# A fused decode block: five attention steps as a loop on TensorE, loads of half the size, and a sigmoid made of exponentials

## The chip, the cores and the metric

The kernel runs on one core of a Trainium2 chip. The metric is the device time of one execution in microseconds; three runs are made and the median is taken.

## The reference

One token for each of two batch rows goes through a layer norm and then through two branches, which are multiplied:

```python
B, D = 2, 448;  Hq, Hkv, Sk, Dh = 16, 8, 4096, 256;  F = 1792

xn = layernorm(x)
q  = (xn @ wq) as 16 heads of 256
p  = softmax(q @ k_cache^T / 16)            # 2 query heads share one of 8 K/V heads
s  = (p @ v_cache) as one row of 4096 @ wo
g  = silu(((xn @ w_gate) * (xn @ w_up)) @ w_down)
out = x + s * g
```

Everything is float32. The K and V caches are 67 MB each, and the five weight matrices some 24 MB together.

## The kernel before

There are 16 attention steps, one for each pair of a K/V head `g` and a batch row `b` (step `i` has `g, b = divmod(i, 2)`). A step reads 4.19 MB of K and 4.19 MB of V. The host lays these out so that a step is 128 rows (partitions) of 8192 numbers of each, 32 KB a row.

**The work of a step.** `scores(i)` makes 16 products on TensorE (32 matmul instructions in the profile) and leaves 128 x 1024 scores in a pair of PSUM banks `s`. `softmax(i)` takes the maximum on VectorE (`m`), turns it by two small products through the PSUM bank `sm` into a maximum for each head (`mx`), subtracts it in an exponential on ScalarE (`p`, with the sum in `su`), and transposes the result on VectorE (`pT`). `values(i)` makes 16 products of `pT` with V into the PSUM bank `o`, and VectorE copies them to `ob`. The order of the steps on TensorE is values(i), scores(i+1), the small products of softmax(i+1), then values(i+1). `combine`, `divide`, `turn` and `project` bring `ob` through the output weights; `total` adds the sums of the softmax.

**The loads.** All are issued on SyncE's queue (SP) in the order of `plan`. `ring` has two buffers of 64 KB a partition, `slot` holds one set of weights. V of step i and K of step i+1 are one load, `vk[i]`, of 128 rows of 64 KB (8.39 MB), and go to the two buffers in turn. A load into a buffer waits until TensorE has read what was there: the load of step i+2 waits for scores(i+1). Between them come the weights: `wgu` behind step 0, `wdq` behind step 2, `wo` behind step 8. At the end come `last0` (K of step 15 and V of step 14, two loads of 32 KB rows) and `last1` (V of step 15 and the rest of `wo`, seven pieces).

**The other branch.** `ffn_in` and `ffn_out` follow steps 0 and 2. The gate is `y * sigmoid(y)`, with ScalarE's sigmoid.

**The order of the instructions.** `Flow` records every operation with what it reads and writes. `settle` works out which earlier operations each has to wait for, and `issue` writes all of them out, unrolled, each engine in the order of the record, with one semaphore per engine and one per load. All instructions thus have one line, 164, in the profile, and groups are told apart by their tiles.

Of the kernel before, what the change touches and what calls it, by code (L numbers as in the profile page):

```python
# [4 lines left out]
AF = mybir.ActivationFunctionType  # L5
OP = mybir.AluOpType
AX = mybir.AxisListType

B, D = 2, 448
# [17 lines left out]
EXTRA = 2 * NS + 1  # L27
LEFT = 64 - NS * SIDE
EPS = 1e-5


class Flow:
# [6 lines left out]
    def __init__(self, nc):  # L39
        self.nc = nc  # L40
        self.ops = []
        self.touched = {}
        self.engines = dict(PE=nc.tensor, DVE=nc.vector, ACT=nc.scalar, POOL=nc.gpsimd, SP=nc.sync)

    def __getattr__(self, engine):
        return Recorder(self, engine)
# [13 lines left out]
        return box[0] // 32 * 32, -(-box[1] // 32) * 32, box[2] // 512 * 512, -(-box[3] // 512) * 512  # L60

    def record(self, engine, call, writes, reads, dma=False):
        op = dict(engine=engine, call=call, needs=set(), wanted=False, dma=dma)
        at = len(self.ops)
        for ap, write in [(a, False) for a in reads] + [(a, True) for a in writes]:
            if ap.tensor.name not in self.touched:
                continue
            psum = ap.space == bass.MemoryType.PSUM
            for other, its, wrote in self.touched[ap.tensor.name]:
                o = self.ops[other]  # L70
                box = self.region(ap)
                alone = psum and o["engine"] != engine
                if alone:
                    box, its = self.shared(box), self.shared(its)
                if not (write or wrote or alone) or box[0] >= its[1] or its[0] >= box[1] or box[2] >= its[3]                         or its[2] >= box[3]:
                    continue
                if o["engine"] == engine and not o["dma"] and (engine == "PE" or not wrote):
                    continue
                op["needs"].add(other)
        for ap, write in [(a, False) for a in reads] + [(a, True) for a in writes]:  # L80
            log = self.touched.setdefault(ap.tensor.name, [])
            box = self.region(ap)
            if write:
                log[:] = [(o, b, w) for o, b, w in log
                          if not (box[0] <= b[0] and b[1] <= box[1] and box[2] <= b[2] and b[3] <= box[3])]
            log.append((at, box, write))
        self.ops.append(op)
        return at

    def settle(self):  # L90

        known = {e: {} for e in self.engines}
        count = {e: 0 for e in self.engines}
        for at, op in enumerate(self.ops):
            e = op["engine"]
            count[e] += 1
            op["lane"], op["n"] = (("dma", at), 1) if op["dma"] else (e, count[e])
            need = [self.ops[o] for o in sorted(op["needs"], reverse=True)]
            waits = {}
            for o in need:  # L100
                if known[e].get(o["lane"], 0) < o["n"]:
                    if any(w["knew"].get(o["lane"], 0) >= o["n"] for w in waits.values()):
                        continue
                    if o["lane"] not in waits or waits[o["lane"]]["n"] < o["n"]:
                        waits[o["lane"]] = o
            waits = {k: o for k, o in waits.items()
                     if not any(w is not o and w["knew"].get(k, 0) >= o["n"] for w in waits.values())}
            for o in waits.values():
                for k, n in o["knew"].items():
                    known[e][k] = max(known[e].get(k, 0), n)  # L110
                o["wanted"] = True
            op["waits"] = sorted(waits.values(), key=lambda o: o["lane"] == e)
            op["knew"] = {**known[e], op["lane"]: op["n"]}

    def issue(self, final):
        nc = self.nc
        self.settle()
        sems = {}
        for op in self.ops:
            if op["wanted"] and op["lane"] not in sems:  # L120
                sems[op["lane"]] = nc.alloc_semaphore(f"s{len(sems)}")
        done = nc.alloc_semaphore("done")
        marks = {}
        for op in self.ops:
            e = op["engine"]
            waits = [(sems[o["lane"]], o["mark"]) for o in op["waits"]]
            while len(waits) > 1:
                gate = self.engines[e].wait_ge(*waits.pop(0))
                if len(waits) > 1:
                    gate.wait_op(*waits.pop(0), "sem-ge")  # L130
            if op is self.ops[-1]:
                for w in waits:
                    self.engines[e].wait_ge(*w)
                op["call"]().then_inc(done, 16)
                nums = sorted(s.num for s in sems.values())
                assert nums == list(range(nums[0], nums[-1] + 1))
                self.engines[e].sem_clear(range(nums[0], nums[-1] + 1))
                self.engines[e].wait_ge(done, 16)
                self.engines[e].sem_clear(done)
                break  # L140
            made = op["call"]()
            for w in waits:
                made.wait_op(*w, "sem-ge")
            if op["wanted"]:
                step = 16 if op["dma"] else 1
                marks[op["lane"]] = op["mark"] = marks.get(op["lane"], 0) + step
                made.then_inc(sems[op["lane"]], step)


class Recorder:  # L150
# [14 lines left out]
        return add  # L165


def gated_decode_block(nc, x, first, vk, last0, last1, wq0, wqx, wdq, wo, wgu, out):
    flow = Flow(nc)
    PE, DVE, ACT, POOL, SP = [getattr(flow, e) for e in ("PE", "DVE", "ACT", "POOL", "SP")]  # L170
    names = iter(range(1000))
# [58 lines left out]
    plan("wq0", wq0)  # L230
    plan("k0", first)
    weights = {0: ("wg wu", wgu), 2: ("wd wq1", wdq), 8: ("wo", wo)}
    for i in range(LAST):
        plan(f"v{i} k{i + 1}", vk[i])
        if i in weights:
            plan(*weights[i])
# [157 lines left out]
    def ffn_out():  # L394
        ps = bank()
        for i in range(14):
            t = i % NT
            PE.matmul(ps[W * t:W * (t + 1), :D], hT[:, i], loaded["wd"][:, i * D:(i + 1) * D],
                             start=i < NT, stop=i >= 14 - NT)
        y = bank()  # L400
        spread(lift(ps), y, True, True)
        e = work["h"]()[:, :SL]
        ACT.activation(e, y[:, :SL], AF.Sigmoid)
        DVE.tensor_mul(gate, y[:, :SL], e)


    def scores(i):
        g, b = divmod(i, B)
        k = loaded[f"k{i}"].rearrange("p (h d c n) -> p h d c n", h=2, d=2, c=NT)
        q = qT[g // 4][:, b, g % 4].rearrange("p d r j -> p d (r j)")  # L410
        m = work["m"]()
        s = two()
        for h in range(2):
            for d in range(2):
                for c in range(NT):
                    PE.matmul(s[W * c:W * (c + 1), h, :], q[:, d], k[:, h, d, c, :], start=d == 0, stop=d == 1)
        DVE.tensor_reduce(m[:, 0:1], s, axis=AX.XY, op=OP.max)
        return s, m


    su = sbuf([128, N], "su")
# [2 lines left out]
        g, b = divmod(i, B)  # L424
        return b * 4 + g if g < 4 else 8 + (b * 3 + g - 4 if i < LAST else 6 + b)

    def softmax(i, s, m, pT=None):
        sm = bank("sm")
        PE.transpose(sm[:1, :128], m[:, 0:1], ident)
        mx = work["mx"]()  # L430
# [10 lines left out]
        return pT  # L441

    over = sbuf([128, N], "over")

    def total(lo, hi, add):

# [54 lines left out]
    ob = work["ob"]()  # L501
    oT0 = sbuf([128, 4, 2, REP, W], "oT0")
    oT2 = sbuf([128, 1, 2, REP, W], "oT2")
    ss = scores(0)
    issue(2)
    p = softmax(0, *ss)
    for i in range(LAST):
        g, b = divmod(i, B)
        o = bank("o")
        values(i, p, o)  # L510
        ss = scores(i + 1)

        issue(1 + (i + 1 in weights))
        DVE.tensor_copy(ob[:, place(i) % 8], o)
        if i == LAST - 1:
            total(8, 14, add_head)
            cb = combine(ob, 6)
        p = softmax(i + 1, *ss)
        if i == 7:
            total(0, 8, add_head)  # L520
            cb = combine(ob, 8)
            for n in range(B):
                turn(oT0, divide(cb[:, n * 256:(n + 1) * 256], 4 * n, 4 * n + 4), 0, n, 4)
            ob = work["ob"]()
        if i in (0, 2, 4, 8):
            if i == 0:
                ffn_in()
            if i == 2:
                ffn_out()
            if i == 4:  # L530
                query(1)
            if i == 8:
                project(oT0, 0, 0, EARLY)

    for n in range(B):
        turn(oT1, divide(cb[:, n * 192:(n + 1) * 192], 8 + 3 * n, 11 + 3 * n), 0, n, 3)
    ss = scores(LAST + 1)
    ps = [p]
    project(oT1, 4, EARLY, LATE)

    last = slot()
    p = softmax(LAST + 1, *ss, last[:, :1024].rearrange("p (h n) -> p h n", h=2))
    o = bank("o")
    values(LAST, ps[0], o)
    ps.append(p)
# [17 lines left out]
    DVE.tensor_mul(gate, acc[:, :SL], gate)  # L563
    DVE.tensor_add(gate, gate, xg)
    SP.dma_start(out, gate)
    flow.issue(out)


# [52 lines left out]
```

## Time and profile before

| | |
|---|---|
| median of 3 runs | 375.16 us (374.98 to 375.22) |
| the profiled execution, its time | 374.99 us |
| the profiled execution, its span | 373.7 us |
| TensorE busy with matmuls | 192.1 us (51%), 1388 matmuls and as many weight loads |
| VectorE, ScalarE, GpSimd busy | 72.9 us (19%), 25.9 us (7%), 1.7 us |
| HBM read | 158.56 MB, 424 GB/s over the span |
| granted TensorE clock, mean | 0.776 |

Times in a row of the timeline or of the chain are the start from the beginning of the span and the duration, both in us; behind `x` stands the number of instructions that are put together in the row, and in brackets the idle time of the engine before it and what ended it. In the rows of waits stand the total, the number and the longest. In the rows of loads stand the number, the size of one, and the median time from issue to landing.

### The profile page before, as it was taken

How to read it: one execution, taken by the hardware profiler on the slowest of the kernel's cores; microseconds unless marked ns; L12 is line 12 of the kernel's file. 1: busy time of each engine (PE TensorE's matmuls, PEld its weight loads, DVE VectorE, ACT ScalarE, POOL GpSimd, SP SyncE). 2: the span in 40 equal slices, each digit the busy share in tenths (PEclk: the TensorE clock that was granted, in tenths of full speed). 3: DMA queues.
4: the chain of work that ended last, by engine and by line, in shares of the span. 5: the costliest groups of instructions: out<-in, count | busy, mean ns of one | idle time of the engine just before them, and what ended most of it. 6: DMA issues, size and time to landing. Idle time of an engine off the chain costs nothing.

```text
span 373.7 us, 3019 instructions
## 1 busy us (share of the span) xinstructions
PE 192.1 (51%) x1388; PEld 50.8 (14%) x1388; DVE 72.9 (19%) x125; ACT 25.9 (7%) x40; POOL 1.7 (0%) x9
## 2 busy tenths in 40 slices
PE   0781468082645091848173656601718090808685
PEld 0220112020111020212010111100202020202122
DVE  2303021104040004050404050400211203030530
ACT  1001010001021001010101010100010101010121
POOL 0100000000000000000000000000000000000000
PEclk9988587667588576798867696985958676877999
DMA  8999899999999999999999999999999999999995
GB/s 322 449 480 435 375 441 449 449 437 433 392 475 435 442 407 428 437 435 442 442 437 428 428 430 422 455 437 435 428 428 428 430 442 449 437 389 431 428 413 221
DMA packets 4217, 158.81 MB, mean 425 GB/s; under 512 B 599, under 2 KB 857, under 8 KB 1241
## 3 DMA queue, kind: packets, MB, share of 16 engines
q1 hardware_dynamic: 4201, 158.62, 98.4%
q8 instruction: 11, 0.18, 0.2%
q14 instruction: 1, 0.01, 0.0%
q10 hardware_dynamic: 4, 0.00, 0.0%
HBM read 158.56 MB, written 0.06 MB: 424 GB/s over the span
## 4 chain that ended last, share of the span: by engine, by line
DMA 75%; PE 22%; DVE 1%; issue 0%; ACT 0%; POOL 0%; ACTq 0%; DVEq 0%
DMA ring<-vk 68%; PE s L164 11%; PE o L164 10%; DMA ring<-last 6%; DMA p<-x 2%; DVE pT L164 0%; DVE qT L164 0%; DVE st L164 0%; DVE oT L164 0%; PE wide L164 0%; ACT ob L164 0%; PE cb L164 0%; DVE gate L164 0%; POOL rstd L164 0%; ACTq L164 0%
## 5 line engine op out<-in xcount | busy, mean ns | idle before, releaser
L164 PE MATMUL o<-ring,pT 128*32 128x512 f32 x480 | 82.5, 850 | 121.4 <-DMA ring<-vk 121.4
L164 DVE TENSOR_REDUCE m<-s 128x1 f32<-128x1024 f32 x16 | 19.6, 1222 | 226.9 <-PE s L164 226.9
L164 PE MATMUL s<-ring,qT 128*32 128x512 f32 x512 | 59.5, 607 | 1.1 <-DVE qT L164 1.1
L164 PEld LDWEIGHTS o<-ring,pT 128*32 128x32 f32 x480 | 18.5, 149 | 175.8 <-DMA ring<-vk 125.8
L164 ACT ACTIVATE p<-s,m 128x1024 f32<-128x1024 f32 x16 | 17.8, 1116 | 321.0 <-DVE m L164 321.0
L164 DVE STREAM_TRANSPOSE pT<-p 128x1024 f32<-128x1024 f32 x15 | 18.7, 1245 | 19.1 <-ACT p L164 19.1
L164 PEld LDWEIGHTS s<-ring,qT 128*32 128x32 f32 x512 | 16.1, 112 | 41.5 <-issue 39.5
L164 PE MATMUL s<-slot,xnT 128*32 128x512 f32 (+1 forms) x96 | 14.4, 751 | 2.3 <-DMA slot<-wgu 2.3
L164 PE MATMUL sm<-ident,m 128*1 128x128 f32 x16 | 4.3, 270 | 19.0 <-DVE m L164 19.0
L164 DVE TENSOR_REDUCE mx<-sm 1x128 f32<-1x512 f32 x16 | 10.7, 670 | 2.9 <-PE sm L164 2.9
L164 PE MATMUL sm<-one,mx 1*128 1x1 f32 x16 | 3.7, 231 | 14.2 <-DVE mx L164 14.2
L164 DVE COPY ob<-o 128x512 f32<-128x512 f32 x14 | 9.5, 681 | 0.0
L164 PE MATMUL s<-slot,oT 20*32 20x512 f32 (+3 forms) x28 | 7.9, 593 | 0.0
L164 PE MATMUL s<-slot,hT 128*32 128x448 f32 x28 | 5.0, 827 | 3.1 <-DMA slot<-wdq 3.1
L164 PE MATMUL s<-ident,pT 2*128 2x2 f32 (+2 forms) x8 | 0.7, 203 | 10.4 <-DVE pT L164 10.4
L164 PEld LDWEIGHTS sm<-ident,m 128*1 128x1 f32 x16 | 1.3, 79 | 33.0 <-DVE m L164 32.4
L164 PE MATMUL wide<-slot,oT 128*32 128x448 f32 x48 | 4.9, 543 | 1.4 <-DMA slot<-wo 0.9
L164 PE MATMUL cb<-ob,add_blocks 128*32 128x512 f32 (+2 forms) x48 | 4.1, 456 | 2.4 <-DVE ob L164 1.6
L164 PE MATMUL s<-ring,slot 128*32 128x512 f32 x32 | 4.2, 600 | 1.7 <-DMA ring<-last 1.7
L164 PEld LDWEIGHTS s<-slot,xnT 128*32 128x32 f32 x96 | 3.3, 137 | 10.4 <-issue 8.0
L164 PEld LDWEIGHTS sm<-one,mx 1*128 1x128 f32 x16 | 2.4, 147 | 17.2 <-DVE mx L164 17.2
L164 ACT ACT_TABLE_LOAD x3 | 3.8, 1283 | 1.6 <-PEq L613 1.6
(63 smaller groups left out, 39.7 us busy)
## 6 DMA issues: line engine op xcount, KB each, us to landing
ring<-last SPq DMA_DIRECT2D x2, 4096.0 KB, 27.5
slot<-wdq SPq DMA_DIRECT2D x1, 6720.0 KB, 46.3
slot<-wgu SPq DMA_DIRECT2D x1, 6272.0 KB, 34.5
slot<-wo SPq DMA_DIRECT2D x1, 5376.0 KB, 41.3
ring<-first SPq DMA_DIRECT2D x1, 4096.0 KB, 20.7
slot<-wq SPq DMA_DIRECT2D x1, 3328.0 KB, 10.8
ring<-last SPq DMA_DIRECT2D x1, 2048.0 KB, 20.4
ring<-last SPq DMA_DIRECT2D x1, 1536.0 KB, 22.4
```

Source lines behind the costliest of these rows:

```text
L164: self.flow.record(self.engine, lambda: method(out, *args, **kw), writes, reads, name == "dma_start")
```

## The change

Steps 9 to 13 (`TURNS`) become five turns of a loop on TensorE. The other engines keep their unrolled code. Four things follow from it:

- An instruction in a loop has fixed addresses, so V and K of these steps always go to the same two halves of one `ring` buffer, in two loads of 32 KB rows each (`late`); V may be loaded once values of the step before are done, K once the scores before are done. The scores always go to one pair of PSUM banks, the maximum to `steady`, and ScalarE copies the query to `qc`.
- Waits within a turn become semaphores of their own (gates): TensorE waits for them in instructions of their own and counts them down again. What the first turn needs from ahead of the loop is awaited before it.
- `softmax(i)` is moved from the end of the step before to the head of the turn. For step 9 this puts it behind `project(oT0, ...)`, and `total` and `combine` after step 13 come ahead of softmax(14). After the loop, `two()` gives scores(15) the pair of banks that held the scores of the loop.
- `SLOT = 0` sets the loop's first instruction at the beginning of a block of 256 instructions.

Apart from the loop, the sigmoid is computed as `y * exp(min(y, 0)) / (1 + exp(-|y|))`, so that ScalarE uses no function but the exponential.

The core of the diff:

```diff
+TURNS = range(9, 14)
+SLOT = 0
...
+        def put(op):
+            engine = self.engines[op["engine"]]
+            await_all(engine, op["waits"][:-1])
+            for gate, n in op["gates"]:
+                engine.wait_ge(gate, n).then_inc(gate, -n)
             made = op["call"]()
...
+            elif name == "PE":
+                for op in todo:
+                    if op["turn"] is None:
+                        put(op)
+                    elif op is mine[0][0]:
+                        await_all(engine, self.ahead)
+                        with nc.Fori(0, len(mine), engines=[mybir.EngineType.PE], head_slot={mybir.EngineType.PE: SLOT}):
+                            for o in mine[0]:
+                                put(o)
...
-        e = work["h"]()[:, :SL]
-        ACT.activation(e, y[:, :SL], AF.Sigmoid)
-        DVE.tensor_mul(gate, y[:, :SL], e)
+        e = work["h"]()
+        up, low = e[:, :SL], e[:, SL:2 * SL]
+        DVE.tensor_scalar(up, y[:, :SL], 0.0, None, op0=OP.min)
+        DVE.scalar_tensor_tensor(low, up, 2.0, y[:, :SL], op0=OP.mult, op1=OP.subtract)
+        ACT.activation(e[:, :2 * SL], e[:, :2 * SL], AF.Exp)
+        DVE.tensor_scalar(low, low, 1.0, None, op0=OP.add)
+        DVE.reciprocal(low, low)
+        DVE.tensor_mul(gate, y[:, :SL], up)
+        DVE.tensor_mul(gate, gate, low)
...
-    for i in range(LAST):
-        g, b = divmod(i, B)
+    for i in range(TURNS[0]):
         o = bank("o")
         values(i, p, o)
-        ss = scores(i + 1)
-
-        issue(1 + (i + 1 in weights))
+        s = scores(i + 1, query_of(i + 1), two() if i + 1 < TURNS[0] else pairs[0])
+        issue(min(1 + (i + 1 in weights), len(todo) - 2))
         DVE.tensor_copy(ob[:, place(i) % 8], o)
...
+    tile = ring()
+    for i in TURNS:
+        flow.turn = i
+        at = 2 * (i - TURNS[0])
+        loaded[f"v{i}"], loaded[f"k{i + 1}"] = tile[:, :ROW], tile[:, ROW:]
+        p = softmax(i, s)
+        SP.dma_start(loaded[f"v{i}"], late[at])
+        o = bank("o")
+        values(i, p, o)
+        DVE.tensor_copy(ob[:, place(i) % 8], o)
+        SP.dma_start(loaded[f"k{i + 1}"], late[at + 1])
+        ACT.copy(qc, query_of(i + 1))
+        scores(i + 1, qc, s)
+    flow.turn = None
+    issue(2)
+    total(8, 14, add_head)
+    cb = combine(ob, 6)
+    p = softmax(LAST, s)
     for n in range(B):
         turn(oT1, divide(cb[:, n * 192:(n + 1) * 192], 8 + 3 * n, 11 + 3 * n), 0, n, 3)
-    ss = scores(LAST + 1)
+    s = scores(LAST + 1, query_of(LAST + 1), two())
```

More of the change, by code (lines that the diff above doesn't have):

```diff
@@ L42, in __init__ @@
         self.touched = {}
-        self.engines = dict(PE=nc.tensor, DVE=nc.vector, ACT=nc.scalar, POOL=nc.gpsimd, SP=nc.sync)
+        self.turn = None
+        self.engines = dict(POOL=nc.gpsimd, DVE=nc.vector, ACT=nc.scalar, SP=nc.sync, PE=nc.tensor)
     def __getattr__(self, engine):
@@ L62, in record @@
     def record(self, engine, call, writes, reads, dma=False):
-        op = dict(engine=engine, call=call, needs=set(), wanted=False, dma=dma)
         at = len(self.ops)
+        op = dict(engine=engine, call=call, needs=set(), wanted=False, dma=dma, turn=self.turn, gates=[])
+        op["place"] = engine, sum(o["turn"] == self.turn and o["engine"] == engine for o in self.ops) if self.turn is not None else at
         for ap, write in [(a, False) for a in reads] + [(a, True) for a in writes]:
@@ L110, in settle, with loop @@
                     known[e][k] = max(known[e].get(k, 0), n)
-                o["wanted"] = True
             op["waits"] = sorted(waits.values(), key=lambda o: o["lane"] == e)
             op["knew"] = {**known[e], op["lane"]: op["n"]}
-    def issue(self, final):
+    def loop(self):
+        turns = sorted({o["turn"] for o in self.ops if o["turn"] is not None})
+        mine = [[o for o in self.ops if o["engine"] == "PE" and o["turn"] == t] for t in turns]
+        by = {(o["turn"], *o["place"]): o for o in self.ops if o["turn"] is not None}
+        self.ahead = []
+        for n, same in enumerate(zip(*mine)):
+            gates = {o["place"] for op in same[1:] for o in op["waits"]}
+            assert all(o["turn"] == op["turn"] for op in same[1:] for o in op["waits"])
+            self.ahead += [o for o in same[0]["waits"] if o["place"] not in gates or o["turn"] != turns[0]]
+            for op in same:
+                op["waits"] = []
+            for place in sorted(gates):
+                gate = self.nc.alloc_semaphore(f"gate{n}{place[0]}{place[1]}")
+                sources = [by[(t, *place)] for t in turns]
+                same[0]["gates"].append((gate, 16 if sources[0]["dma"] else 1))
+                for o in sources:
+                    assert "gate" not in o
+                    o["gate"] = gate
+        assert all(o["turn"] is None for o in self.ahead)
+        for op in self.ops:
+            for o in op["waits"]:
+                o["wanted"] = True
+        for o in self.ahead:
+            o["wanted"] = True
+        for same in zip(*mine):
+            for op in same:
+                op["wanted"] = any(o["wanted"] for o in same)
+        return mine
@@ L116, in issue @@
+    def issue(self):
         nc = self.nc
+        first = nc.alloc_semaphore("first").num
         self.settle()
-        sems = {}
+        mine = self.loop()
+        sems, marks = {}, {}
         for op in self.ops:
-            if op["wanted"] and op["lane"] not in sems:
-                sems[op["lane"]] = nc.alloc_semaphore(f"s{len(sems)}")
-        done = nc.alloc_semaphore("done")
[L123 to L129, printed above, removed]
-                    gate.wait_op(*waits.pop(0), "sem-ge")
[L131 to L140, printed above, removed]
-            made = op["call"]()
[L142 to L147, printed above, removed]
@@ new lines, in issue, with await_all @@
+            if op["wanted"]:
+                assert "gate" not in op
+                if op["lane"] not in sems:
+                    sems[op["lane"]] = nc.alloc_semaphore(f"s{len(sems)}")
+                op["step"] = 16 if op["dma"] else 1
+                marks[op["lane"]] = op["mark"] = marks.get(op["lane"], 0) + op["step"]
+        done = nc.alloc_semaphore("done")
+        def await_all(engine, waits):
+            waits = [(sems[o["lane"]], o["mark"]) for o in waits]
+            while waits:
+                gate = engine.wait_ge(*waits.pop(0))
+                if waits:
+                    gate.wait_op(*waits.pop(0), "sem-ge")
@@ new lines, in put @@
+        def put(op):
[3 more added lines that the diff above has]
+                engine.wait_ge(gate, n).then_inc(gate, -n)
+            made = op["call"]()
+            for o in op["waits"][-1:]:
+                made.wait_op(sems[o["lane"]], o["mark"], "sem-ge")
+            if "gate" in op:
+                made.then_inc(op["gate"], 16 if op["dma"] else 1)
+            elif op["wanted"]:
+                made.then_inc(sems[op["lane"]], op["step"])
@@ new lines, in issue @@
+        store = self.ops.pop()
+        for name, engine in self.engines.items():
+            todo = [o for o in self.ops if o["engine"] == name]
+            if name == "SP":
+                for op in todo:
+                    put(op)
+                await_all(engine, store["waits"])
+                store["call"]().then_inc(done, 16)
+                engine.sem_clear(range(first, done.num))
+                engine.wait_ge(done, 16)
+                engine.sem_clear(done)
+            elif name == "PE":
+                for op in todo:
+                    if op["turn"] is None:
+                        put(op)
+                    elif op is mine[0][0]:
[3 more added lines that the diff above has]
+                                put(o)
+            else:
+                for op in todo:
+                    put(op)
@@ L165, in __getattr__, with gated_decode_block @@
         return add
-def gated_decode_block(nc, x, first, vk, last0, last1, wq0, wqx, wdq, wo, wgu, out):
+def gated_decode_block(nc, x, first, vk, late, last0, last1, wq0, wqx, wdq, wo, wgu, out):
     flow = Flow(nc)
@@ L401, in ffn_out, with query_of, scores @@
         spread(lift(ps), y, True, True)
-        e = work["h"]()[:, :SL]
-        ACT.activation(e, y[:, :SL], AF.Sigmoid)
-        DVE.tensor_mul(gate, y[:, :SL], e)
-    def scores(i):
+        e = work["h"]()
[7 more added lines that the diff above has]
+        DVE.tensor_mul(gate, gate, low)
+    def query_of(i):
         g, b = divmod(i, B)
+        return qT[g // 4][:, b, g % 4].rearrange("p d r j -> p d (r j)")
+    def scores(i, q, s):
         k = loaded[f"k{i}"].rearrange("p (h d c n) -> p h d c n", h=2, d=2, c=NT)
-        q = qT[g // 4][:, b, g % 4].rearrange("p d r j -> p d (r j)")
-        m = work["m"]()
-        s = two()
         for h in range(2):
@@ L416, in scores @@
                     PE.matmul(s[W * c:W * (c + 1), h, :], q[:, d], k[:, h, d, c, :], start=d == 0, stop=d == 1)
-        DVE.tensor_reduce(m[:, 0:1], s, axis=AX.XY, op=OP.max)
-        return s, m
+        return s
     su = sbuf([128, N], "su")
@@ L425, in place, with softmax @@
         return b * 4 + g if g < 4 else 8 + (b * 3 + g - 4 if i < LAST else 6 + b)
-    def softmax(i, s, m, pT=None):
+    def softmax(i, s, pT=None):
+        m = steady if i in TURNS else work["m"]()
+        DVE.tensor_reduce(m[:, 0:1], s, axis=AX.XY, op=OP.max)
         sm = bank("sm")
@@ L443, in gated_decode_block @@
     over = sbuf([128, N], "over")
+    steady = sbuf([128, 2], "steady")
+    qc = sbuf([128, 2, W], "qc")
     def total(lo, hi, add):
@@ L503, in gated_decode_block @@
     oT2 = sbuf([128, 1, 2, REP, W], "oT2")
-    ss = scores(0)
+    s = scores(0, query_of(0), two())
     issue(2)
-    p = softmax(0, *ss)
-    for i in range(LAST):
-        g, b = divmod(i, B)
+    p = softmax(0, s)
+    for i in range(TURNS[0]):
         o = bank("o")
         values(i, p, o)
-        ss = scores(i + 1)
-        issue(1 + (i + 1 in weights))
+        s = scores(i + 1, query_of(i + 1), two() if i + 1 < TURNS[0] else pairs[0])
+        issue(min(1 + (i + 1 in weights), len(todo) - 2))
         DVE.tensor_copy(ob[:, place(i) % 8], o)
[L515 to L518, printed above, removed]
+        if i + 1 < TURNS[0]:
+            p = softmax(i + 1, s)
         if i == 7:
@@ L524, in gated_decode_block @@
             ob = work["ob"]()
[L525 to L533, printed above, removed]
+        if i == 0:
+            ffn_in()
+        if i == 2:
+            ffn_out()
+        if i == 4:
+            query(1)
+        if i == 8:
+            project(oT0, 0, 0, EARLY)
+    tile = ring()
[16 more added lines that the diff above has]
+    p = softmax(LAST, s)
     for n in range(B):
         turn(oT1, divide(cb[:, n * 192:(n + 1) * 192], 8 + 3 * n, 11 + 3 * n), 0, n, 3)
-    ss = scores(LAST + 1)
+    s = scores(LAST + 1, query_of(LAST + 1), two())
     ps = [p]
@@ L541, in gated_decode_block @@
     last = slot()
-    p = softmax(LAST + 1, *ss, last[:, :1024].rearrange("p (h n) -> p h n", h=2))
+    p = softmax(LAST + 1, s, last[:, :1024].rearrange("p (h n) -> p h n", h=2))
     o = bank("o")
@@ L565, in gated_decode_block @@
     SP.dma_start(out, gate)
-    flow.issue(out)
+    flow.issue()
 def kernel(A_x, A_k_cache, A_v_cache, A_wq, A_wo, B_x, B_w_gate, B_w_up, B_w_down):
@@ L582 @@
     first = c(k[0])
-    vk = np.concatenate([v[:n], k[1:n + 1]], 2)
+    early = TURNS[0]
+    vk = np.concatenate([v[:early], k[1:early + 1]], 2)
+    late = np.stack([v[early:n], k[early + 1:n + 1]], 1).reshape(-1, 128, ROW)
     last = [np.concatenate([k[n + 1], v[n]], 1), v[n + 1]]
@@ L613 @@
     nc = bacc.Bacc("TRN2", target_bir_lowering=False, num_devices=1, dynamic_dma_scratch_size=1024)
-    arrays = dict(x=x, first=first, vk=vk, last0=last[0], last1=last[1], wq0=wq0, wqx=wqx, wdq=wdq, wo=wo, wgu=wgu)
+    arrays = dict(x=x, first=first, vk=vk, late=late, last0=last[0], last1=last[1], wq0=wq0, wqx=wqx, wdq=wdq, wo=wo, wgu=wgu)
     args = [nc.dram_tensor(n, a.shape, mybir.dt.from_np(a.dtype), kind="ExternalInput").ap()
```

## The prediction, made before the result was known

> **What bounds the kernel now.** I read the page first, then the waits of the DMA queue, then the chain of waits in order of time, then the timeline of a few steps.
>
> ```profile
> span 373.7 us, 3019 instructions
> PE 192.1 (51%) x1388; PEld 50.8 (14%) x1388; DVE 72.9 (19%) x125; ACT 25.9 (7%) x40; POOL 1.7 (0%) x9
> DMA  8999899999999999999999999999999999999995
> q1 hardware_dynamic: 4201, 158.62, 98.4%
> q8 instruction: 11, 0.18, 0.2%
> DMA 75%; PE 22%; DVE 1%; issue 0%; ACT 0%; POOL 0%; ACTq 0%; DVEq 0%
> ```
>
> The 16 DMA engines are busy for 98.4% of the span with q1, the loads of weights and cache, and the row of tenths has no hole. The loads move 158.6 MB, every input once. The edit can win only by making those engines do less, and it can lose only by letting them run dry or by lengthening the end after the last load.
>
> ```profile
> SPq L164 <- PE s L164: 303.1, 17, 34.3
> PE o L164 <- DMA ring<-vk: 121.4, 14, 16.1
> 76.32 6.26 PE o L164 x32
> 131.39 6.04 PE o L164 x32
> 259.91 4.93 PE o L164 x32
> 264.84 3.48 PE s L164 x32
> 268.34 30.14 DMA ring<-vk
> 279.21 5.52 PE L164 MATMUL o<-ring,pT 128*32 128x512 f32 x32 [8.18 <-DMA ring<-vk]
> 298.53 6.09 PE o L164 x32
> 317.85 4.97 PE L164 MATMUL o<-ring,pT 128*32 128x512 f32 x32 [6.99 <-DMA ring<-vk]
> 337.65 5.35 PE o L164 x32
> ```
>
> The issuing queue waits for TensorE to free a buffer, and TensorE waits for loads. Which of the two is the bound shows in the steps. The starts of values(9) to values(13) (the `o` rows) are 19.30, 19.32, 19.32 and 19.80 us apart, and each starts when its load lands, whatever its own work took (4.93 to 6.09 us). The load for the step after next is issued once scores are done (268.34) and lands 30.14 us later, so about 10 us of that it lies in the queue behind its predecessor. That reserve is what the edit spends.
>
> **The change part by part.**
>
> *Loads in halves, one place for each of V and K.* Five loads of 8.39 MB in 64 KB rows become ten of 4.19 MB in 32 KB rows; the bytes are the same. At 19.32 us a pair, one lands every 9.66 us. Rows of 32 KB are already there, in the two halves of k15 and v14:
>
> ```profile
> 322.89 0.33 SPq L164 DMA_DIRECT2D ring<-last  x1
> 326.32 0.33 SPq L164 DMA_DIRECT2D ring<-last  x1
> ring<-last SPq DMA_DIRECT2D x2, 4096.0 KB, 27.5
> res<-gate SPq DMA_DIRECT2D x1, 56.0 KB, 1.6
> slot<-wdq SPq DMA_DIRECT2D x1, 6720.0 KB, 46.3
> ```
>
> The median of two is their mean, so they land at 352.1 on average. At 9.66 us each behind the load that landed at 337.6 they would land at 347.3 and 357.0, mean 352.1. So 32 KB rows run at the pace of 64 KB rows, to the 0.05 us of these rows; over five turns that is between -0.3 and +0.3 us, and I take +0.1. Five more issues of 0.33 us cost SP nothing, since it waits 303.1 us.
>
> The Trainium skill ("DMA: Bandwidth & Descriptors", "Anatomy of one DMA") speaks against smaller loads: each DMA has a fixed cost of about 2.0 us beside its bytes. If none of it overlapped, five more loads would add 10 us by that page. The two halves above show none of it, because the second was in the queue before the first was done.
>
> So each load must still be queued before the one ahead of it ends. The smallest load with nothing ahead of it, `res`, takes 1.6 us from issue to landing; I use that as the start-up. The order on SP is v, k, v, k. v(i+1) overwrites v(i), so it waits for values(i); k(i+2) waits for scores(i+1). Take t = 0 as the landing of K of a turn. V of the turn lands at 9.66, the next K at 19.32, so the next V has to be issued by 19.32 - 1.6 = 17.72. What comes before is scores, softmax, values:
>
> ```profile
> 23.55 5.37 PE s L164 x32
> 217.09 1.23 DVE L164 TENSOR_REDUCE m<-s 128x1 f32<-128x1024 f32 x1 [12.75 <-PE s L164]
> 218.37 0.27 PE L164 MATMUL sm<-ident,m 128*1 128x128 f32 x1 [1.36 <-DVE m L164]
> 221.24 1.25 DVE L164 STREAM_TRANSPOSE pT<-p 128x1024 f32<-128x1024 f32 x1 [1.27 <-ACT p L164]
> ```
>
> Scores take 3.48 us behind a running burst, and 5.37 when they start one (23.55). Softmax takes 217.09 to 222.49, 5.40. Values take 4.93 to 6.26. From t = 0 the V place is free at 9.66 + 4.93 = 14.6 at the earliest, and at 5.37 + 5.40 + 6.26 = 17.03 at the latest: 3.1 to 0.7 us to spare, less a few tenths for the separate waits and the branch that TensorE's sequencer now runs in each turn. For K the reserve is 9.66 - 1.6 - 5.37 = 2.7 us. The copy of the query to one place on ScalarE waits for nothing late: it lies between the exponential and the landing of the next K. Only v11, v12 and v13 are this tight: v9 and k10 go into a place that is free early, and v10 waits for values(9), whose weights are ready long before its V. So no idle time in the queue: 0.
>
> *Softmax(9) goes behind the projection with wo.*
>
> ```profile
> 240.57 3.21 PE L164 MATMUL wide<-slot,oT 128*32 128x448 f32 x32 [0.92 <-DMA slot<-wo]
> ```
>
> The projection ends at 243.8. The transposes of the maxima follow it, and p is ready some 4.1 us later (218.4 to 222.5 in the step above), at 247.9. V of step 9 lands at 240.57 + 9.66 = 250.2 and covers it, with 2.3 us left, also for a jump into the loop. Without that cover values(9) would be late, and it has until 259.9 - 1.6 before anything follows from it.
>
> *The end.* last0 is issued right behind k14, before the queue is empty, and the first piece of last1 waits for values(13), which now comes earlier, V having landed 9.66 us ahead of K.
>
> ```profile
> 343.00 22.42 DMA ring<-last
> 365.46 2.30 PE s L164 x16
> 350.96 3.64 PE L164 MATMUL s<-ring,qT 128*32 128x512 f32 x32
> 351.26 1.12 ACT L164 ACTIVATE p<-s,m 128x1024 f32<-128x1024 f32 x1 [20.82 <-DVE m L164]
> ```
>
> There is one new wait: scores(15) now writes the PSUM pair that the exponential of step 14 reads (in the code, `two()` after the loop hands out the pair of the loop). It started at 350.96, before that exponential ended at 352.38, so it would come 1.4 us later. But scores(14) no longer stand behind values(13): they start with K's landing near 337.65 instead of 343.0, and everything up to that exponential moves up by 3.5 to 5.3 us. The last loads (365.46) still end last: 0.
>
> *Sigmoid from exponentials.*
>
> ```profile
> 110.46 1.28 ACT L164 ACT_TABLE_LOAD   x1
> 118.30 0.27 ACT L164 ACTIVATE h<-s 128x112 f32<-128x112 f32 x1 [6.55 <-PE s L164]
> 118.58 1.28 ACT L164 ACT_TABLE_LOAD   x1
> 118.60 0.27 DVE L164 TENSOR_TENSOR gate<-s,h 128x112 f32<-128x112 f32 x1 [0.82 <-ACT h L164]
> ```
>
> Two table loads of 1.28 us go; five more VectorE operations of about 0.27 us come, 1.4 us. TensorE waits for its load until 131.39 anyway, so both are worth 0.
>
> *Instruction loads.* TensorE has 2776 of the 3019 instructions and q8 made 11 loads, one per some 250. Four unrolled turns of about 132 instructions go, so two loads fewer. A load is 0.2% of 16 x 373.7 us over 11, about 1.1 us on one DMA engine. A step ends with its slowest DMA engine, so most loads of instructions cost nothing, and one that meets the slowest delays all. The step from 317.85 to 337.65 is 0.48 us longer than its neighbours, and I take it for such a meeting, which the rows do not prove. Bounds: -1.1 (both removed loads met the slowest) to 0. I take -0.4.
>
> Sum: 0.1 + 0 + 0 + 0 - 0.4 = -0.3 us. The profiled execution took 374.99 us (its span of 373.7 and 1.3 around it) and the median of the runs is 375.16; 374.99 - 0.3 = 374.7 and 375.16 - 0.3 = 374.9, so I say 374.8. A measurement of this kernel tells 0.2% (0.75 us) from no change, and this is less.
>
> **The rivals.**
>
> *V comes late (slower).* If scores and values both start their bursts slowly, and the loop's own waits add more than the 0.7 us left, SP issues V after K has ended and the DMA engines stand still, in the turns of v11, v12 and v13. For it: both bursts now start after idle time, where before scores followed values at 3.48 us. Against it: values done early leave the gap before K, values done late close it. Values run 4.93 to 6.26; a burst all at the pace of the slow matmuls (the slowest values, 6.26, plus as much again as scores lost at 23.55, 1.9, in both bursts) would be free at 5.37 + 5.40 + 8.2 = 19.0, 1.2 us late. It decides from 17.72 on. Price: 0.3 to 1.5 us in each of three turns, 1 to 4.5 us; time 376 to 379.5, middle 377. At its far end every one of the ten loads starts in an empty queue, 10 x 1.6 = 16 us, 391 us: chance 0.01.
>
> *The branch back loads instructions again.* The body of some 140 instructions is less than the 250 of one load, so it should stay. If not, each turn adds a load of 1.1 us on one DMA engine and as long a stall of TensorE, which eats the 0.7 us left. Price: 0 to 1.1 us by the DMA engine, up to 0.4 a turn by the stall: 375.2 to 377, middle 376. In the trace of before no branch is taken, so nothing speaks for or against. The Trainium skill ("Runtime: NRT & Kernel Launch", "Instruction fetch mechanics") says that code comes in blocks of 256 instructions, and that a taken branch stalls for a DMA when its target lies outside the window of blocks at hand. The 11 loads for 2776 agree with blocks of that size.
>
> *More is won.* From 76.32 to 131.39 two pairs and the 6720 KB of wdq (6.88 MB) were loaded; at 19.32 us for 8.39 MB that is 54.5 us, and it took 55.1. If that excess too goes with the different code, the gain is 0.48 + 0.6: 374.0. For it: the code of all engines is laid out anew. Against it: it lies ahead of the loop.
>
> *The loop changes nothing in the loads* (as many, or they meet other engines): 375.2.
>
> **How the numbers follow.** Forecast 0.45; changes nothing 0.18; more is won 0.13; V late 0.13 with its far end; branch 0.11. The likeliest time is 374.8. Range: from 374.1, just above "more is won", to 377.0, which takes in the branch and half of V late. Faster by over 0.2% (below 374.4): more is won and 0.10 of the forecast, 0.23. Slower (above 375.9): V late 0.13 and 0.06 of the branch, with 0.02 of the rest, 0.21. Same: 0.56.
>
> **What would show it.** Right: the DMA row still without a hole; values in the turns starting at the landing of V, V and K landing 9.7 us apart; nine q8 loads; one table load; the last wait still for `last`. V late: values in turns 11 to 13 released by VectorE's pT, and a wait of TensorE for K of over 20 us from the one before. Branch: 13 or more q8 loads, and gaps on TensorE at the head of each turn. The prediction is wrong if the DMA share of the stretch from 260 to 340 us falls below its neighbours, or if the wait at the end is no longer for a load.

## The result: slower by 1.4%, and the profile after

The changed kernel takes 380.36 us (median of 6 runs, 378.32 to 381.49), the kernel before 375.11 us in its 6 runs. The ratio is 1.0135, with a 95% interval of 1.0107 to 1.0164. The profiled execution took 381.04 us, with a span of 379.8 us against 373.7.

The page of the changed kernel, its first part and its queues:

```profile
span 379.8 us, 3071 instructions
DMA  8999999999999999999999999999999999999995
q1 hardware_dynamic: 4921, 158.62, 97.9%
q8 instruction: 9, 0.15, 0.1%
```

The bytes are the same, q1's share of the longer span is lower, and the row of tenths shows no hole: each slice is 9.5 us long and a gap of one or two us stays a 9. Shares of the spans give a first account of the 6.1 us: the packets of q1 took 97.9% of 379.8 = 371.8 us, before 98.4% of 373.7 = 367.7 us, so 2.0 us are time without packets and 4.1 us are packets that took longer. The same four steps as a whole, before and after (window, length, busy time and number of TensorE, its weight loads, VectorE, ScalarE and GpSimd, granted clock, DMA share, GB/s):

```profile
259.90:337.65 77.75, 37.24 (x264) 9.57 (x265) 15.24 (x20) 4.83 (x8) 0.00 (x0) 0.74 0.99 430
260.38:343.63 83.25, 44.66 (x264) 12.39 (x265) 15.98 (x20) 5.35 (x12) 0.00 (x0) 0.76 0.98 407
```

The DMA share hardly moves, the rate falls from 430 to 407 GB/s. The stretches from one start of scores to the next, each one turn, show more, in the same columns:

```profile
260.38:281.67 21.29, 12.52 (x66) 3.19 (x67) 4.00 (x5) 1.34 (x3) 0.00 (x0) 0.70 0.95 388
281.67:302.74 21.07, 9.69 (x66) 2.74 (x67) 4.00 (x5) 1.34 (x3) 0.00 (x0) 0.84 0.99 411
302.74:323.25 20.51, 11.24 (x67) 3.24 (x68) 4.00 (x5) 1.34 (x3) 0.00 (x0) 0.75 0.99 409
323.25:343.63 20.38, 11.22 (x66) 3.22 (x67) 4.00 (x5) 1.34 (x3) 0.00 (x0) 0.75 0.99 421
```

A turn should take the 19.32 us of its loads. These take 1.97, 1.75, 1.19 and 1.06 us more, 5.97 in all, and the span grew by 6.1. So the whole loss lies in these four turns. The timeline, with the first turns in more detail and the issues of V:

```profile
250.72 6.25 PE L224 MATMUL o<-ring,pT 128*32 128x512 f32 x32 [5.31 <-PEq L176]
257.06 0.33 SPq L224 DMA_DIRECT2D ring<-late  x1
260.38 6.54 PE L224 MATMUL s<-ring,qc 128*32 128x512 f32 x32 [3.41 <-PEq L176]
266.99 1.23 DVE L224 TENSOR_REDUCE steady<-s 128x1 f32<-128x1024 f32 x1 [9.24 <-PE s L224]
271.15 1.25 DVE L224 STREAM_TRANSPOSE pT<-p 128x1024 f32<-128x1024 f32 x1 [1.27 <-ACT p L224]
272.69 5.51 PE L224 MATMUL o<-ring,pT 128*32 128x512 f32 x32 [3.01 <-PEq L176]
278.29 0.33 SPq L224 DMA_DIRECT2D ring<-late  x1
281.67 3.64 PE L224 MATMUL s<-ring,qc 128*32 128x512 f32 x32 [3.46 <-PEq L176]
298.70 0.33 SPq L224 DMA_DIRECT2D ring<-late  x1
302.74 5.34 PE L224 MATMUL s<-ring,qc 128*32 128x512 f32 x32 [4.13 <-PEq L176]
319.37 0.33 SPq L224 DMA_DIRECT2D ring<-late  x1
323.25 5.34 PE L224 MATMUL s<-ring,qc 128*32 128x512 f32 x32 [3.97 <-PEq L176]
343.63 5.34 PE L224 MATMUL s<-ring,qc 128*32 128x512 f32 x32 [3.86 <-PEq L176]
```

Scores start when K has landed, values when V has landed and the softmax is done, and `PEq` is the sequencer's separate wait for either. V was issued 3.3, 3.4, 4.0 and 3.9 us before the scores started, so before K, the load ahead of it, had landed. This time, from the issue of a load to the landing of the load ahead of it, is called its reserve. The turn that began there lost 1.97, 1.75, 1.19 and 1.06 us. Reserve and loss add up to 5.3, 5.1, 5.2 and 4.9 us.

The rows of loads, taken for each V by itself, give its landing (the last number is the time from issue to landing):

```profile
ring<-late SPq DMA_DIRECT2D x1, 4096.0 KB, 14.5
ring<-late SPq DMA_DIRECT2D x1, 4096.0 KB, 14.6
ring<-late SPq DMA_DIRECT2D x1, 4096.0 KB, 14.7
ring<-late SPq DMA_DIRECT2D x1, 4096.0 KB, 14.3
```

V thus lands 11.2, 11.2, 10.7 and 10.4 us behind K instead of 9.66. That is 4.8 of the 5.97 us; the rest falls to the K loads, which had 4.6 to 7.5 us of reserve. The theory for the experiments, "reserve", is: **a load must be issued about 5 us before the landing of the load ahead of it, and what is missing is lost.**

### The profile page after: what moved, and what is told of

It is laid out like the page before. It is cut to its first block, busy times and chain, and to the rows that moved or that the text cites. A ratio compares the mean times of both kernels' runs of the same rounds, so it can differ in the third digit from the quotient of the medians.

```text
span 379.8 us, 3071 instructions
## 1 busy us (share of the span) xinstructions
PE 206.8 (54%) x1388; PEld 55.6 (15%) x1388; DVE 77.2 (20%) x130; ACT 24.0 (6%) x43; POOL 1.7 (0%) x9
## 3 DMA queue, kind: packets, MB, share of 16 engines
q1 hardware_dynamic: 4921, 158.62, 97.9%
## 5 line engine op out<-in xcount | busy, mean ns | idle before, releaser
L224 PE MATMUL o<-ring,pT 128*32 128x512 f32 x480 | 86.7, 889 | 95.5 <-DMA ring<-vk 73.1
L224 PE MATMUL s<-ring,qT 128*32 128x512 f32 x352 | 41.4, 614 | 2.7 <-ACT p L224 1.6
L224 PE MATMUL s<-ring,qc 128*32 128x512 f32 x160 | 26.2, 814 | 18.8 <-PEq L176 18.8
L224 ACT ACTIVATE p<-s,m 128x1024 f32<-128x1024 f32 x11 | 12.2, 1113 | 217.6 <-DVE m L224 217.6
L224 DVE TENSOR_REDUCE m<-s 128x1 f32<-128x1024 f32 x11 | 13.4, 1221 | 28.7 <-PE s L224 28.7
L224 PE MATMUL s<-slot,xnT 128*32 128x512 f32 (+1 forms) x96 | 16.4, 840 | 2.4 <-DMA slot<-wgu 2.4
L224 PEld LDWEIGHTS s<-ring,qT 128*32 128x32 f32 x352 | 11.5, 113 | 31.2 <-issue 27.6
L224 DVE TENSOR_REDUCE steady<-s 128x1 f32<-128x1024 f32 x5 | 6.1, 1224 | 35.7 <-PE s L224 35.7
L224 PEld LDWEIGHTS s<-ring,qc 128*32 128x32 f32 x160 | 7.5, 141 | 36.9 <-issue 36.9
L224 ACT ACTIVATE p<-s,steady 128x1024 f32<-128x1024 f32 x5 | 5.6, 1114 | 104.9 <-DVE steady L224 104.9
## 6 DMA issues: line engine op xcount, KB each, us to landing
ring<-late SPq DMA_DIRECT2D x10, 4096.0 KB, 14.8
```

The lines of the kernel that those rows point to most:

```text
L224: self.flow.record(self.engine, lambda: method(out, *args, **kw), writes, reads, name == "dma_start")
```

## The experiments

### Undo one part: the loop, the one place, the size

The first edit writes the five turns out and keeps all else:

```diff
     for i in TURNS:
-        flow.turn = i
```

> The five turns are written out instead of looped; V and K keep their one place and their 32 KB rows. In the profile of the changed kernel each of the loads v10 to k14 lands late by about 4.9 us less the time that it was issued ahead of its predecessor's landing. Theory 'reserve' (a load has to be issued about 4.9 us before the load ahead of it has landed, what is missing is lost): the places stay, so the time stays at 378 to 381.5 us. Rival 'loop' (gates, branch and the code of the loop cost about 1.2 us a turn): 375 us. Rival 'size' (32 KB rows cost 0.6 us a load by themselves): 378 to 381.5 us too.

Measured: 379.01 us (378.74 to 380.52), ratio 1.0117 (1.0091 to 1.0143). Without the loop the kernel is slow as well, and the two intervals overlap. The last turn of its profile, the issue of V and the scores:

```profile
316.61 0.33 SPq L224 DMA_DIRECT2D ring<-late  x1
320.26 6.19 PE L224 MATMUL s<-ring,qc 128*32 128x512 f32 x32 [3.71 <-DMA ring<-late]
341.44 5.34 PE L224 MATMUL s<-ring,qc 128*32 128x512 f32 x32 [4.06 <-DMA ring<-late]
```

Here too 3.65 us of reserve, and 21.18 us for the turn, 1.86 lost. The three turns before it had 4.3, 3.7 and 3.5 us of reserve and lost 0.5, 0.7 and 1.1 us, so reserve and loss add up to between 4.4 and 5.5 us.

The second edit adds two buffers to that one, and keeps the ten loads of 32 KB rows:

```diff
-    tile = ring()
     for i in TURNS:
+        tile = ring()
```

> Written out, with V and K still as ten loads of 32 KB rows, but in the two buffers in turn as before. 'Reserve': each load is issued over 10 us ahead, 374.9 to 375.8 us. 'Loop': 375 us as well. 'Size': 378 to 381.5 us.

Measured: 375.11 us (374.81 to 376.13), ratio 1.0003 (0.9993 to 1.0013). So neither the size of the loads nor their rows cost anything that can be measured; with the first edit this leaves the one place.

The third keeps loop and place, and lets go of a buffer earlier:

```diff
-        SP.dma_start(loaded[f"v{i}"], late[at])
+        for h in range(2):
+            cut = slice(h * ROW // 2, (h + 1) * ROW // 2)
+            SP.dma_start(loaded[f"v{i}"][:, cut], late[at][:, cut])
...                                     # K likewise
```

> The loop stays, and V and K stay in one place, but each is loaded as two halves of 16 KB rows, so that the first half is issued once half of the values (or scores) are done. 'Reserve': the first half of V is issued some 2.7 us earlier (3.3 to 3.9 us ahead become about 6), the second half has a landing 4.8 us later to go by (about 8), so no load is late: 374.5 to 375.8 us. 'Loop': unchanged, 378 to 381.5 us. 'Size': twenty loads instead of ten, 384 us or more.

Measured: 375.36 us (375.25 to 375.5), ratio 1.0007 (0.9997 to 1.0017). Its profile, the issue of V's first half in a turn and the starts of the second half of the scores (which wait for K's second half):

```profile
273.07 0.33 SPq L224 DMA_DIRECT2D ring<-late  x1
279.63 3.22 PE L224 MATMUL s<-ring,qc 128*32 128x512 f32 x16 [2.93 <-PEq L176]
299.09 1.92 PE L224 MATMUL s<-ring,qc 128*32 128x512 f32 x16 [2.59 <-PEq L176]
```

The reserve is 6.6 us and the turn takes 19.46. Doubling the number of loads took the loss away, which no price per load can explain.

The fourth is a loop that keeps the two buffers: two turns of two steps each, with one load of 64 KB rows a step.

```diff
-TURNS = range(9, 14)
+TURNS = range(10, 14)
...
-    tile = ring()
+    tiles = [ring(), ring()]
+    sides = pairs[:]
     for i in TURNS:
-        flow.turn = i
+        flow.turn = i // 2
+        tile = tiles[i % 2]
...
-        SP.dma_start(loaded[f"v{i}"], late[at])
+        SP.dma_start(tile, late[i - TURNS[0]])
...
-        SP.dma_start(loaded[f"k{i + 1}"], late[at + 1])
...
-        scores(i + 1, qc, s)
+        s = scores(i + 1, qc, sides[(i + 1) % 2])
```

> A loop on TensorE (two turns of two steps each, steps 10 to 13, the body of some 280 instructions from the beginning of a block) with V and K of a step as one load of 64 KB rows, in the two buffers in turn as before; the exponentials stay. 'Reserve': each load is issued 10 us ahead, so the loop's own waits and its branch are hidden and nothing is lost: 374.5 to 375.6 us, with fewer instruction loads than the 11 of before. 'Loop': 1.2 us a turn of one step, about 379 us.

Measured: 374.91 us (374.73 to 375.62), ratio 0.9995 (0.9985 to 1.0004): the loop costs nothing here, and gains nothing. Its instruction loads, from the page, and the last starts of values, from the timeline:

```profile
q8 instruction: 10, 0.16, 0.2%
```

```profile
279.48 6.49 PE L224 MATMUL o<-ring,pT 128*32 128x512 f32 x32 [7.20 <-PEq L176]
298.80 5.37 PE L224 MATMUL o<-ring,pT 128*32 128x512 f32 x32 [6.64 <-PEq L176]
318.74 5.64 PE L224 MATMUL o<-ring,pT 128*32 128x512 f32 x32 [8.38 <-PEq L176]
338.04 6.23 PE L224 MATMUL o<-ring,pT 128*32 128x512 f32 x32 [7.47 <-PEq L176]
```

One instruction load fewer, and still one step of 19.94 us among those of 19.3.

### The sigmoid alone

The kernel before with only the new lines of the gate from the diff.

> The kernel before with nothing changed but the gate's sigmoid, made of exponentials. Two ScalarE table loads go, five small VectorE operations come, all while TensorE waits for a load. Every theory: no difference, 374.7 to 375.4 us. If the table loads had mattered, up to 2.6 us less.

Measured: 374.97 us, ratio 0.9997 (0.9986 to 1.0008): nothing.

### Take away what makes V late

In the loop, scores and values start after idle time and run slowly. Products that nothing uses fill that time:

```diff
+    def busy(n):
+        for _ in range(n):
+            PE.matmul(bank("cb")[:, :128], ident, add_head.rearrange("p a r j -> p (a r j)"), start=True, stop=True)
...
+        busy(12)
         o = bank("o")
         values(i, p, o)
         DVE.tensor_copy(ob[:, place(i) % 8], o)
+        busy(20)
```

> The changed kernel with small products added that nothing uses, in the loop's idle times of TensorE: 20 behind the values and 12 behind the softmax's own. They are to keep the granted clock up, so that scores and values take some 3.5 us instead of 5.3 to 6.5. 'Reserve': V is then issued about 2 us earlier, some 5.5 us ahead instead of 3.3 to 3.9, and K some 6 us ahead, so that little or nothing is lost: 374.9 to 376.5 us. If the slow bursts have no part in it, the time stays at 378 to 381.5 us.

Measured: 375.63 us (375.03 to 376.36), ratio 1.0012 (1.0000 to 1.0023). The stretches of two turns, and from the timeline the values of a turn and the issue of V behind them:

```profile
260.31:279.66 19.35, 15.28 (x131) 9.76 (x131) 4.00 (x5) 1.34 (x3) 0.00 (x0) 1.00 1.00 427
279.66:299.03 19.37, 16.79 (x130) 11.16 (x131) 4.00 (x5) 1.34 (x3) 0.00 (x0) 0.91 1.00 431
```

```profile
269.98 3.64 PE L224 MATMUL o<-ring,pT 128*32 128x512 f32 x32 [0.40 <-PEq L176]
273.70 0.33 SPq L224 DMA_DIRECT2D ring<-late  x1
```

The granted clock is 1.00 and 0.91 instead of 0.70 to 0.84, the bursts take 3.64 us instead of mostly 5.3 to 6.5, V is issued 6.0 us ahead, and a turn takes 19.35 us. More work on TensorE made the kernel 4.7 us faster. In the main this fits the Trainium skill ("TensorE: Matmul & The Clock Gate", "What's actually happening"), by which the clock falls to half after an idle window of about 3.4 us: the waits ahead of the bursts in the changed kernel are 3.0 to 5.3 us, and all but one of these bursts are slow (the scores at 281.67 came after 3.46 us and took 3.64), while the waits ahead of them here are 1.4 us and less.

### The reserve measured in the kernel before

The kernel before, unrolled and with its two buffers, with single loads issued later by a chain of GpSimd fills between the last read of the buffer and the issue. Three kernels differ only in which loads are delayed and in the number of fills:

```diff
+    def flow_delay(t, n):
+        POOL.memset(t[:, :1], 0.0)
+        POOL.memset(t[:, ROW:ROW + 1], 0.0)
+        POOL.memset(t[:, 2 * ROW - 1:2 * ROW], 0.0)
+        for _ in range(n):
+            POOL.memset(scratch, 0.0)
+        POOL.memset(t[:, :1], 0.0)
```

> The kernel before with nothing changed but the moment at which seven of its 8.39 MB loads are issued: a chain of 10 to 60 small GpSimd fills of some 0.2 to 0.4 us each lies between the last read of the buffer and the issue. It gives the loss of a load as a function of how far ahead of its predecessor's landing it is issued. 'Reserve': no loss down to about 5 us ahead, below that the landing comes later by 4.9 us less the reserve, whatever the size of the rows. If the start-up is the 1.6 us that the prediction used, losses begin only at 1.6 us.

> The kernel before again with six of its 8.39 MB loads issued later, by 13 to 22 GpSimd fills of 0.26 us, which should leave about 5.9, 5.1, 4.6, 4.9, 4.4 and 3.6 us between the issue and the landing of the load ahead. In the first such run a reserve of 4.1 us lost 0.2 us, 3.8 lost 1.1, 2.9 lost 2.4 and 2.8 lost 1.1. 'Reserve' with a threshold near 5 us: nothing above 5, a few tenths at 4.4 to 4.9, about 1 us at 3.6; some 2 us in all, 376 to 378 us. If the loss has no threshold there but grows from a larger reserve on, the first two lose as well and the time is above 378 us.

> The kernel before again with loads issued later, now so late that the queue is nearly or wholly empty: about 3 us ahead of the landing of the load before (twice), 0 to 1 us ahead (once), and 2 to 3 us after it (twice). If each late issue costs what is missing of 5 us, whatever the queue holds, the loads at 3 us ahead lose about 2 us and those at 2 to 3 us after lose 7 to 8. If a queue that is wholly empty starts all its engines at once, as one such load did in the first of these runs (9.1 us lost at 5.1 us after, thus 4.0 us from issue on beside the 19.32 of the bytes, one instruction load among them), those lose 5 to 6 only.

Measured, one execution each: 388.78, 375.73 and 389.18 us. Values start when their load has landed, so the start of values is the landing. From the first kernel (four rows), the second (three) and the third (three), issues and starts of values:

```profile
277.90 0.33 SPq L165 DMA_DIRECT2D ring<-vk  x1
280.80 5.14 PE L165 MATMUL o<-ring,pT 128*32 128x512 f32 x32 [6.80 <-DMA ring<-vk]
302.55 6.21 PE L165 MATMUL o<-ring,pT 128*32 128x512 f32 x32 [10.41 <-DMA ring<-vk]
351.44 5.66 PE L165 MATMUL o<-ring,pT 128*32 128x512 f32 x32 [15.99 <-DMA ring<-vk]
```

```profile
274.31 0.33 SPq L165 DMA_DIRECT2D ring<-vk  x1
279.54 6.62 PE L165 MATMUL o<-ring,pT 128*32 128x512 f32 x32 [7.04 <-DMA ring<-vk]
298.86 5.50 PE L165 MATMUL o<-ring,pT 128*32 128x512 f32 x32 [6.51 <-DMA ring<-vk]
```

```profile
306.08 4.50 PE L165 MATMUL o<-ring,pT 128*32 128x512 f32 x20 [7.49 <-DMA ring<-vk]
309.06 0.33 SPq L165 DMA_DIRECT2D ring<-vk  x1
330.85 5.78 PE L165 MATMUL o<-ring,pT 128*32 128x512 f32 x32 [12.31 <-DMA ring<-vk]
```

In the first, a load issued 2.90 us before 280.80 landed at 302.55, 21.75 us later: 2.43 lost. In the second, one issued 5.23 us ahead came after 19.32 us: nothing lost. In the third, one issued 2.98 us after the landing at 306.08 came 24.77 us after that landing: 5.45 lost. All issues of the three with less than 6 us of reserve, in the same way (negative: issued after the landing, into an empty queue):

| reserve, us | 5.5 | 5.5 | 5.2 | 5.2 | 5.0 | 4.1 | 4.1 | 4.1 | 3.8 | 2.9 | 2.8 | 1.9 | -1.3 | -3.0 | -5.1 |
|---|---|---|---|---|---|---|---|---|---|---|---|---|---|---|---|
| lost, us | 0 | 0 | 0 | 0 | 1.4 | 0.2 | 0.7 | 0 | 1.1 | 2.4 | 1.1 | 2.0 | 5.2 | 5.4 | 9.1 |

Above 5.1 us nothing is lost. Below 4 every load loses, and reserve and loss add up to 3.9 to 5.3 us; into an empty queue they add up to 2.5 to 4.0. Between 4 and 5 us it is open in each case. The losses of a kernel add up to 13.9, 0.7 and 14.0 us; it took 13.8, 0.8 and 14.4 us longer than the kernel before measured beside it. So the threshold belongs to neither the loop nor the halves, since this kernel has neither. It is softer than the theory had it: three loads at 4.1 us lost 0.2, 0.7 and 0, and one at 5.0 lost 1.4. That the second kernel lost less than expected says nothing against the theory: most of its reserves came out longer than planned, and only one of its six loads had less than 5.2 us. For the queue that is wholly empty the third expectation's second case holds: those two loads lost 5.2 and 5.4 us, not 7 to 8 (the first was issued 1.3 us after the landing, earlier than planned).

## Why the prediction was wrong

The forecast was 374.8 us, no change; the measured time lies above its range. The rival "V comes late", which had a chance of 0.13, happened, and its range of 376 to 379.5 us ended below the 380.36 measured. Its picture of DMA engines that stand still is a third of it: 2.0 us are idle, and 4.1 us are packets that took longer. The sign by which the prediction wanted to know itself wrong, a lower DMA share between 260 and 340 us, hardly shows it: 0.98 against 0.99, and below 0.99 in the first turn only.

**The step that failed is the start-up of 1.6 us.** It was read from `res`, which the prediction calls a load. It is the store of the result, 56 KB in rows of 448 bytes, and its time was used for loads of 4 MB. The runs show 2.5 to 4.0 us beside the bytes in an empty queue, and some 5 us of reserve behind a running load. With 5 in place of 1.6 the deadline for V moves from 17.72 to 14.3 us after K's landing, and the prediction's own earliest time, 14.6, already misses it.

**The chain to V was sized nearly right.** Predicted were 14.6 to 17.0 us plus a few tenths; from the scores' starts to V's issues it was 17.9, 17.0 and 16.6 us. The first of these is beyond the bound: scores there took 6.54 us, where the bound of 5.37 was one burst from the beginning of the trace.

**The bound on the loss was short for a second reason.** The rival's price per turn (0.3 to 1.5 us) came from the same 1.6. What a turn lost was 1.06 to 1.97 us, and in four turns, not three: v10, in the first of them, was called safe because values(9) have their weights early. But they took 6.25 us from V's landing (250.72), and the issue at 257.06 left 3.3 us.

**Right:** the bytes and their pace (32 KB rows: ratio 1.0003), the sigmoid at 0, the loop's body staying loaded (9 instruction loads as forecast, and the loop alone at ratio 0.9995), and the end. The chain of the changed kernel:

```profile
362.95 6.46 PE o L224 x32
369.73 4.05 PE s L224 x32
377.85 0.27 DVE gate L224
```

Values(14) now start after idle time and take 6.46 us, and values(15) run in one go behind them, so TensorE's last wait for a load is the one for V of step 14. Still the last operation starts 6.0 us later than before (377.85 against 371.81), which is what the four turns lost.

**Not borne out:** the -0.4 us for fewer instruction loads. The loop alone has one load fewer and a long step of 19.94 us all the same, and its gain, if any, is within -0.15% to +0.04%. What makes that step long wasn't tried.

The prediction weighed a fixed cost of 2.0 us for each DMA from the Trainium skill ("DMA: Bandwidth & Descriptors", "Anatomy of one DMA") against the two halves of `last0` and set it aside. That section gives the figure for DMAs that GpSimd issues, and these loads are issued on SyncE's queue. The halves could not tell either: they were issued at 322.89 and 326.32, 14.8 and some 21 us before the loads ahead of them landed (337.65 and, by the prediction's estimate, 347.3). Loads issued into an empty queue needed 2.5 to 4.0 us beside their bytes here.

## What to carry to other kernels

When loads are the bound, a buffer's release time matters as the reserve that it leaves in the queue: subtract the issue from the landing of the load ahead, and compare that with what a load of the same size and direction needs, not with a small store. Two buffers of one load each gave some 10 us here, one place for each of V and K left 3.3 to 4.0, and cutting each load in two, with each half released when it had been read, brought back 6.6 in the same space. The row of tenths shows nothing of such losses, and the DMA share little, since most of the loss was in packets that took longer. The length and the GB/s of stretches laid from landing to landing show it.

## What the runs showed of the hardware

A queue that has run dry does not start a large load in the time of a small store. In the first of the three delayed kernels the load of 351.44 was issued at 328.09, into an empty queue; the stretches behind it (in these windows a packet counts in the one in which it starts, so shares above 1 are many starts):

```profile
328.00:329.00 1.00, 1.00 (x12) 0.31 (x8) 0.00 (x0) 0.00 (x0) 0.06 (x2) 0.88 0.00 0
329.00:330.00 1.00, 1.00 (x16) 0.34 (x12) 0.00 (x0) 0.00 (x0) 0.00 (x0) 1.00 3.09 1049
330.00:331.00 1.00, 1.00 (x16) 0.26 (x12) 0.00 (x0) 0.00 (x0) 0.00 (x0) 1.00 0.00 0
332.00:333.00 1.00, 0.65 (x8) 0.00 (x0) 0.27 (x1) 0.00 (x0) 0.00 (x0) 1.00 2.19 934
334.00:335.00 1.00, 0.27 (x1) 0.08 (x1) 1.00 (x2) 0.00 (x0) 0.00 (x0) 1.00 2.12 918
```

The first 16 packets (64 KB each, one for each DMA engine) start between 0.9 and 1.9 us after the issue. All of them start in one stretch of 1 us, so its share of 3.09 is also their mean time in us. Nearly all of the second ones start from 332 on, and from there a packet takes some 2.4 us, an eighth of the 19.32 us of a load. The late start and the slow first packets account for 1.6 to 2.6 of the 4.0 us that this load needed beside its bytes (an instruction load fell into it too). Slower first packets would also explain why the share stays high while the rate falls in the changed kernel; for its loads of 32 KB rows that was not tried. Why a queue that still holds work for several us needs some 5 us to go on without loss is not settled by these runs.
